# Attention with a gated token-mixing MLP on one core: rebuilding the prologue that leads to the first exponential

## The chip, the cores and the metric

The kernel runs on one core of one Trainium2 chip. The core has a matrix engine (TensorE, PE in the profile), a vector engine (VectorE, DVE), an activation engine (ScalarE, ACT), a general engine (GpSimd, POOL) and a queue engine that issues the transfers (SyncE, SP). The metric is the device time of one launch in microseconds; lower is better. Times given for the kernel are medians of several runs. The profile is one further execution.

## The reference

The input x has 2048 tokens of 640 features. It is normalized, goes through 32-head attention (20 features a head), and is multiplied by the SiLU of an MLP over the token axis, whose input is normalized once more:

```
xn  = layernorm(x)
qkv = xn @ wqkv                       # 32 heads, 20 features each
s   = softmax(q k^T / sqrt(20)) v @ wo
h   = layernorm(xn)                   # the second norm
u   = gelu(h^T @ w1 + b1)             # mixes tokens: 2048 -> 1536
y   = (u @ w2 + b2)^T                 # 1536 -> 2048
out = x + s * silu(y)
```

The scores are 32 x 2048 x 2048 numbers, and each needs an exponential. That is where the time of this kernel goes.

## The kernel before, in words

**Units.** The 32 heads go in eight groups G of four heads. In a group the queries go in four parts p of 512. One pass is one (G, p): 16 key blocks c of 128 keys times 4 heads g, 64 units. A unit is a score tile of 128 keys by 512 queries, so there are 2048 units. Four heads' scores can stand beside each other in TensorE, 32 rows each (L1024). A unit's exponential is taken either by ScalarE, two units at a time (L1051, 128 x 1024), or by VectorE as a chain of six instructions (L1091 to L1097, 128 x 512). The results are multiplied with the values (L1138) into one accumulator bank (bank 6), which a pass owns until its epilogue reads it (L1188). ScalarE's results stand in a ring of 24 tiles (`pt_sb`), VectorE's in one of 8.

**The prologue.** Before any score, x must be normalized. x is held in 16 blocks of 128 tokens, in four groups gb of four blocks. Per block there are two `bn_stats` (L545, L547) and one `bn_aggr` (L550) on VectorE; per group one addition of epsilon (L554) on VectorE, one power -0.5 on GpSimd over four columns (L557), and four normalizing instructions on VectorE (L560). Then TensorE transposes 20 tiles of 128 x 128 (L604) in three jobs of 2, 2 and 1 feature chunks; each job's bank is evicted to `xnT_sb` by VectorE (L949) or ScalarE (L948). With a group's transposed block the projections follow: keys of group G = 0 for 512 tokens (`k0_gb`, L622, evicted at L955 on ScalarE or L956 on VectorE), queries (`q0_0`, later `q0_1` to `q0_3`), and values in two jobs (`v0_...`, L674, evicted at L949). Scores of pass (0, 0) need `q0_0` and the key projection of their key block: each `k0_gb` opens 16 units, which are eight exponentials of ScalarE.

**The second norm.** Its row factor follows from the first one's statistics. Per group, GpSimd does five small instructions over four columns (L572 to L580, the fourth, L578, a power), and VectorE then writes the four blocks of h to `regC` (L583). All four groups do so after the last normalization (`xn_g3`). The MLP's first weights overwrite x in `regA`, so their load (`w1a`) waits for all of h.

**Constants.** VectorE fills the ones columns of the values and the gaps between them (L1213, L1215; `v_ones`), the store buffer `on_sb` (L1216) and a padded output weight (L1217), and writes the padding of the second query and key buffer (L1255), all in the prologue.

**What sets the order.** The instruction order of each engine is fixed when the program is built, by a planner in the same file. Work is given as jobs: a list of steps, the tags that must be done before (`requires`), and a priority (lower goes first). The planner keeps a model clock per engine with a cost for every step, always takes the engine whose next step can start first, and among steps ready then the one with the lowest priority number; evictions (`ev` steps) get 30 off theirs, scores have 0. An eviction may go to VectorE, or to ScalarE as well while the ramp lasts, that is until `v0_15` is done. VectorE's exponentials start only after that. Every engine runs its list strictly in order on the chip, so a step that is late there holds everything behind it.

A job that writes PSUM takes one of seven banks and holds it to its eviction. Once scores can start, banks 0 to 3 belong to ScalarE's exponentials, and three (4, 5, 7) are left to the prologue's jobs; at the end of the ramp 4 and 5 go to VectorE's exponentials. The jobs that want a bank stand in one queue, of which the planner looks at the first four. Later work (the other groups' key and query chunks, the MLP) is released by the number of the unit reached, not by time. Where TensorE would otherwise stand idle the planner puts in dummy multiplications (L1593, L1601).

**Loads.** All go through SP's queue in the order of the program, and rotate over eight lanes, each of which waits for its own transfer before. The first are x blocks 0, 1, 2-3, the first key and query columns, x blocks 4-7, the first value columns, x blocks 8-11 and 12-15 (`dma_x` L466, `dma_w` L471).

**The tail guard.** `DVE_TAIL_GUARD` keeps VectorE off the last units of a pass: it takes none of the last four. The same number sets how many units before the very end VectorE's banks are given up.

```
            if u < NU and u + len(dg) > pass_end[u] - self.DVE_TAIL_GUARD:
                u = pass_end[u]
```

## Time and profile before

| | us |
|---|---|
| median of 5 runs (873.74 to 875.24) | 874.17 |
| the profiled execution | 874.86 |
| its span | 872.7 |
| first exponential on ScalarE starts | 16.57 |
| first exponential step on VectorE starts (L1091) | 54.73 |
| ScalarE busy in the span | 842.5 |
| VectorE busy | 823.6 |
| TensorE busy (ends modelled, overlapping, dummies included) | 801.6 |

Busy time by stage, from the view that cuts the span into windows:

| window, us | TensorE | VectorE | ScalarE | GpSimd | GB/s |
|---|---|---|---|---|---|
| 0 to 5 | 2.83 | 3.81 | 1.28 | 0.74 | 154 |
| 5 to 10 | 3.13 | 3.98 | 0 | 1.02 | 304 |
| 10 to 15 | 4.26 | 4.90 | 2.29 | 0 | 366 |
| 15 to 20 | 4.97 | 3.65 | 3.69 | 1.01 | 197 |
| 20 to 30 | 8.55 | 8.62 | 9.06 | 1.44 | 95 |
| 30 to 40 | 8.57 | 8.20 | 7.34 | 2.70 | 7 |
| 40 to 50 | 8.06 | 8.70 | 7.41 | 6.48 | 2 |
| 50 to 60 | 9.74 | 6.13 | 8.78 | 0 | 197 |
| 60 to 80 | 18.81 | 19.83 | 20.00 | 0 | 29 |
| 800 to 850 | 44.14 | 47.84 | 49.83 | 0 | 26 |

How to read the profile: a group row gives line, engine, operation, output and input by name, shape, count, then busy time, mean nanoseconds of one, and the idle time of the engine just ahead of such instructions with what ended it. Records overlap, because an instruction's record begins before its predecessor's ends, so sums of records are somewhat longer than the engine's pace. In the timeline a row may merge several instructions; it gives start and duration, and in brackets the idle time before it. The chain of waits goes back from the last instruction to what released it each time.

### The profile page before, as it was taken

To read this page: it belongs to the slowest core of one execution; us is meant where nothing else is said; L and a number is where in the kernel's file an instruction comes from. 1 tells how busy PE (TensorE), PEld (TensorE's weight loads), DVE (VectorE), ACT (ScalarE), POOL (GpSimd) and SP (SyncE) were. 2 spreads that over 40 slices of the span, in tenths; PEclk is the share of its full clock that TensorE was granted. 3 is DMA by queue.
4 is the path that set the end of the run, shared out by engine and by line. 5 is a ranking of instruction groups with operands and counts; after the bars stand their busy time and mean duration, and the time that the engine had idled before them with its cause. 6 is when DMAs were issued, how large, how long until landed. Compare 5 with 4: busy or idle time off the path is not lost.

```text
span 872.7 us, 16547 instructions
## 1 busy us (share of the span) xinstructions
PE 801.6 (92%) x5814; PEld 260.0 (30%) x5908; DVE 823.6 (94%) x2048; ACT 842.5 (97%) x915; POOL 13.4 (2%) x31
## 2 busy tenths in 40 slices
PE   7889999999999999999999999999899999999897
PEld 4432222222332323232232223222222222222233
DVE  7979999999999999999999999999999999999997
ACT  4889999999999999999999999999999999999995
POOL 1310000000000000000000000000000000000000
PEclk9999999999999999999999999999999999999999
DMA  8140110010121213020013020222402210032111
GB/s 236 45 106 13 30 36 11 15 31 14 28 63 25 63 32 88 10 60 11 11 25 77 21 51 12 66 47 50 89 15 61 47 12 5 7 101 71 41 34 45
DMA packets 123286, 39.32 MB, mean 45 GB/s; under 512 B 84248, under 2 KB 122088, under 8 KB 123208
## 3 DMA queue, kind: packets, MB, share of 16 engines
q1 hardware_dynamic: 123208, 38.27, 19.2%
q8 instruction: 50, 0.82, 0.4%
q14 instruction: 28, 0.23, 0.1%
HBM read 25.88 MB, written 9.83 MB: 41 GB/s over the span
## 4 chain that ended last, share of the span: by engine, by line
ACT 84%; PE 8%; DVE 5%; POOL 1%; issue 1%; DMA 1%; SPq 0%; ACTq 0%; POOLq 0%; DVEq 0%
ACT pt_sb L1051 82%; PE ps_all L1024 3%; PE ps_all L1138 2%; PE ps_all L798 1%; ACT zt_sb L757 1%; ACT zt_sb L762 1%; POOL st_sb L578 1%; PE ps_all L1593 0%; PE ps_all L1601 0%; DMA regA<-in_A_x_dram 0%; PE ps_all L674 0%; PE ps_all L729 0%; DVE ew_sb L1091 0%; PE ps_all L622 0%; DVE dpt_sb L1097 0%
## 5 line engine op out<-in xcount | busy, mean ns | idle before, releaser
L1051 ACT ACTIVATE pt_sb<-ps_all 128x1024 bf16<-128x1024 f32 x889 | 821.4, 1124 | 7.6 <-PE ps_all L1024 6.8
L1024 PE MATMUL ps_all<-qk_sb 32*128 32x512 bf16 (+1 forms) x2112 | 368.9, 377 | 52.6 <-ACT pt_sb L1051 39.9
L1091 DVE TENSOR_SCALAR ew_sb<-ps_all 128x512 uint16<-128x512 uint16 x271 | 182.9, 684 | 23.8 <-PE ps_all L1024 22.8
L1024 PEld LDWEIGHTS ps_all<-qk_sb 32*128 32x128 bf16 x2112 | 97.7, 91 | 347.2 <-ACT pt_sb L1051 294.8
L1097 DVE SCALAR_TENSOR_TENSOR dpt_sb<-ps_all,el_sb 128x512 uint16<-128x512 f32 x271 | 180.5, 681 | 1.7
L1138 PE MATMUL ps_all<-pt_sb,v_sb 128*32 128x512 bf16 (+1 forms) x1834 | 163.9, 379 | 0.0
L1095 DVE TENSOR_TENSOR el_sb<-ev_sb,el_sb 128x512 bf16<-128x512 bf16 x271 | 109.3, 414 | 0.8
L1096 DVE TENSOR_TENSOR el_sb<-el_sb,ew_sb 128x512 bf16<-128x512 bf16 x271 | 108.8, 414 | 0.7
L1138 PE MATMUL ps_all<-dpt_sb,v_sb 128*32 128x512 bf16 (+1 forms) x278 | 85.4, 379 | 0.0
L729 PE MATMUL ps_all<-regB,regA 128*128 128x128 bf16 (+1 forms) x370 | 74.2, 299 | 2.6 <-issue 1.4
L1092 DVE TENSOR_SCALAR ev_sb<-ew_sb 128x512 bf16<-128x512 uint16 x271 | 74.2, 284 | 2.3
L729 PE MATMUL ps_all<-regC,regA 128*128 128x128 bf16 (+1 forms) x370 | 73.1, 299 | 1.4 <-issue 0.5
L1093 DVE TENSOR_SCALAR el_sb<-ew_sb 128x512 bf16<-128x512 uint16 x271 | 73.7, 282 | 0.0
L641 PE MATMUL ps_all<-xnT_sb,wqk_sb 128*112 128x512 bf16 x200 | 68.2, 405 | 1.0 <-DVE zt_sb L735 0.8
L1138 PEld LDWEIGHTS ps_all<-pt_sb,v_sb 128*32 128x32 bf16 x1834 | 36.6, 94 | 57.1 <-issue 50.0
L1593 PE MATMUL ps_all<-wrm_sb 128*128 128x512 bf16 (+1 forms) x139 | 41.1, 379 | 3.9 <-DVE ps_all L505 2.2
L729 PEld LDWEIGHTS ps_all<-regB,regA 128*128 128x128 bf16 x384 | 26.0, 97 | 38.3 <-issue 24.4
L729 PEld LDWEIGHTS ps_all<-regC,regA 128*128 128x128 bf16 x384 | 25.4, 97 | 38.1 <-issue 29.0
L674 PE MATMUL ps_all<-wv_sb,xnT_sb 128*128 128x160 bf16 (+1 forms) x160 | 34.0, 309 | 0.0
L798 PE MATMUL ps_all<-wo_sb,xnT_sb 128*128 128x128 bf16 (+2 forms) x152 | 30.8, 298 | 1.0 <-issue 0.9
L641 PEld LDWEIGHTS ps_all<-xnT_sb,wqk_sb 128*112 128x112 bf16 x200 | 21.7, 127 | 31.4 <-issue 13.2
L1601 PE MATMUL ps_all<-wrm_sb,v_sb 128*128 128x512 bf16 x76 | 27.2, 386 | 0.5 <-DVE rden_sb L1194 0.2
(79 smaller groups left out, 352.4 us busy)
## 6 DMA issues: line engine op xcount, KB each, us to landing
regA<-in_B_w_dram SPq DMA_DIRECT2D x6, 1024.0 KB
regA<-in_B_w_dram SPq DMA_DIRECT2D x8, 768.0 KB
regA<-in_A_x_dram SPq DMA_DIRECT2D x7, 640.0 KB
qkT_scratch_dram<-pk_sb SPq DMA_DIRECT2D x40, 112.0 KB
qk_sb<-qkT_scratch_dram SPq DMA_DIRECT2D x56, 80.0 KB
on_scratch_dram<-on_sb SPq DMA_DIRECT2D x124, 20.0 KB
out_dram<-regC SPq DMA_DIRECT2D x3, 640.0 KB
wqk_sb<-in_A_wqkv_dram SPq DMA_DIRECT2D x2, 680.0 KB
```

The lines of the kernel that those rows point to most:

```text
L641: steps.append(("pe", lambda e, dc=dc: e.matmul(ps_all[0:112, bk * 512:(bk + 1) * 512], wqk_sb[:, dc * 1280 + c0:dc * 1280 + c0 + 112], xn ...
L729: steps.append(("pe", lambda e, k=k: e.matmul(ps(bk, n), wap[:, k, col0:col0 + 128], rows[:, k, c0:c0 + n], start=(k == 0), stop=(k == nk ...
L1024: pr.pe(lambda e, outp=outp, lhsT=lhsT, rhs=rhs, g=g: e.matmul(outp, lhsT, rhs, start=True, stop=True, tile_position=(32 * g, 0)), reads=[ ...
L1051: tk = pr.act(lambda e: e.activation(outp, inp, AF.Exp, bias=-self.OFFS * math.log(2.0) / 128.0, scale=math.log(2.0) / 128.0), reads=[bank ...
L1091: (lambda e: e.tensor_scalar(w3, lo, 0x7FFF, None, ALU.bitwise_and), bs, [sw], dv(N)),
L1092: (lambda e: e.tensor_scalar(v_, w_, 1.0 / 256.0, -128.0, ALU.mult, ALU.add), [sw], [sv], dv(N, .26)),
L1093: (lambda e: e.tensor_scalar(l_, w_, a3 / 65536.0, (b3 - 64.0 * a3) / 256.0, ALU.mult, ALU.add), [sw], [sl_], dv(N, .26)),
L1095: (lambda e: e.tensor_tensor(l_, v_, l_, ALU.mult), [sv, sl_], [sl_], dv(N, .52)),
L1096: (lambda e: e.tensor_tensor(l_, l_, w_, ALU.mult), [sl_, sw], [sl_], dv(N, .52)),
L1097: (lambda e: e.scalar_tensor_tensor(o_, zr, -(self.OFFS - 16256.0), l_, ALU.add, ALU.add), bs + [sl_], [S_(f"dpt{s0 + i}") for i in range( ...
L1138: pr.pe(lambda e, outp=outp, lhsT=lhsT, rhs=rhs, k=k, g=g: e.matmul(outp, lhsT, rhs, start=(k == 0), stop=(k == NB - 1), tile_position=(0, ...
L1593: pe_full(lambda e: e.matmul(ps(wb, n), wrm_sb[:, 0:P], wrm_sb[:, P:P + n], start=True, stop=True), [S_("warm"), S_("warm1")], [bank_slot[ ...
```

## The change

- **Statistics.** Those of blocks 1 and 5 move to ScalarE (`act_stats`): an Identity with scale -1/640 whose accumulator gives the negative mean, a Square with that as bias whose accumulator gives the sum of squared deviations, and a one-column Copy that divides it by 640. Their element outputs go to `regC` as scrap. Since the mean is negative there, the two blocks' normalizations add it instead of subtracting. The rest of the statistics become jobs of their own (`stat0` to `stat3`), so that a group's statistics no longer wait for the normalization of the group before.
- **Loads.** x blocks 2 and 3 come by two transfers.
- **Group 0.** Its transposes are five jobs: for blocks 0 and 1 four chunks and one, for blocks 2 and 3 two, two and one. Queries 0 to 255 and keys 0 to 127 are projected after the first half, queries 256 to 511 and keys 128 to 511 after the second. The scores of key block 0 wait for all queries and the first key part only. The first value projections require that scores have begun (`STbegin0`).
- **Second norm.** One round of five GpSimd instructions over all 16 columns (`hstat`) instead of four rounds over four; the 16 VectorE writes of h have priority 88 (`H_PRIO`) instead of 32 to 35.
- **Constants.** The six fills go to GpSimd, ahead of all its powers. The padding of the second query and key buffer becomes a job of priority 60 after the last normalization.
- **Planner.** The model's cost of evicting a transposed block on VectorE is 0.55 ns an element instead of 1.04, and those of some small steps change; the tail guard is 3 instead of 4.

The diff, cut to its core:

```diff
     CHUNK_FROM = 44.0
+    ACT_STATS = (1, 5)
+    H_PRIO = 88.0
     DVE_EXP = True
-    DVE_TAIL_GUARD = 4
+    DVE_TAIL_GUARD = 3
     NTMP = 4
...
         dma_x(0, 1)
         dma_x(1, 1)
-        dma_x(2, 2)
+        dma_x(2, 1)
+        dma_x(3, 1)
...
+        def act_stats(b):
+
+            junk = regC[:, b, :]
+            nm, va = st_sb[:, 0, b:b + 1], st_sb[:, 1, b:b + 1]
+            return [("act", lambda e: e.activation(junk, regA[:, b, :], AF.Identity, scale=-1.0 / D, accum_out=nm),
+                     [S_(f"x{b}")], [S_(f"mv{b}"), S_(f"h{b}")], f"as0_{b}", ac(640)),
+                    ("act", lambda e: e.activation(junk, regA[:, b, :], AF.Square, bias=nm, accum_out=va),
+                     [S_(f"x{b}")], [S_(f"mv{b}"), S_(f"h{b}")], f"as1_{b}", ac(640) + 93.0),
+                    ("act", lambda e: e.activation(va, va, AF.Copy, scale=1.0 / D), [], [S_(f"mv{b}")], f"as2_{b}", 200.0)]
...
+        def stat_steps(gb):
+                if b in self.ACT_STATS:
+                    continue
...
+        def hstat_steps():
+
+            mvs = [S_(f"mv{b}") for b in range(NB)]
+            rs = [S_(f"rstd{gb}") for gb in range(4)]
+            sw, s3 = S_("lnw2"), S_("rr")
+            return [
+                ("pool", lambda e: e.tensor_tensor(st(5, 0, NB), st(2, 0, NB), st(2, 0, NB), ALU.mult), rs, [sw], "ha", 250.0),
+                ("pool", lambda e: e.tensor_tensor(st(5, 0, NB), st(5, 0, NB), st(1, 0, NB), ALU.mult), [sw] + mvs, [sw],
+                 "hb", 250.0),
+                ("pool", lambda e: e.tensor_scalar(st(5, 0, NB), st(5, 0, NB), self.EPS, None, ALU.add), [sw], [sw], "hc",
+                 300.0),
+                ("pool", lambda e: e.tensor_tensor(st(6, 0, NB), st(5, 0, NB), mhalf(NB), ALU.pow), [sw, S_("mhalf")],
+                 [S_("r2")], "hd", 1800.0),
+                ("pool", lambda e: e.tensor_tensor(st(3, 0, NB), st(2, 0, NB), st(6, 0, NB), ALU.mult), rs + [S_("r2")],
+                 [s3], "he", 250.0), ("tag", "hstat")]
...
+        def xT0_steps(half, dcs, nm):
+
+            def make(bk):
+                steps = []
+                pb = ps_all[:, bk * 512:(bk + 1) * 512].bitcast(bf)
+                for b in (2 * half, 2 * half + 1):
+                    for i, dc in enumerate(dcs):
+                        outp = pb[:, i * 256 + (b % 2) * 128:i * 256 + (b % 2 + 1) * 128]
+                        steps.append(("pe", lambda e, outp=outp, b=b, dc=dc: e.transpose(
+                            outp, xn_ap(b)[:, dc * 128:(dc + 1) * 128], idb_sb[:]),
+                            [S_(f"xn{b}"), S_("idb")], [bank_slot[bk]], "xT0", 128))
+                n = len(dcs)
+                dst = xnT_sb[:, dcs[0]:dcs[0] + n, half * 256:(half + 1) * 256]
+                src = pb[:, 0:n * 256].rearrange("p (c n) -> p c n", c=n)
+                steps.append(("ev", dst, src, "copy", None, [bank_slot[bk]], [S_(f"xT{dc}_0{half}") for dc in dcs],
+                              "xTe0", n * 256))
+                steps.append(("tag", f"xT0_{nm}"))
+                return steps
+            return make
...
+        def qk0_steps(w, c0, n, half, nm):
+
+            def make(bk):
+                steps = []
+                rd = [S_(f"wp{w}_0")] + [x for dc in range(5) for x in xsl(dc, 0, half)]
+                for dc in range(5):
+                    steps.append(("pe", lambda e, dc=dc: e.matmul(
+                        ps(bk, n), wqk0_sb[:, dc, w, :], xnT_sb[:, dc, c0:c0 + n], start=(dc == 0),
+                        stop=(dc == 4)), rd, [bank_slot[bk]], f"qk0_{w}_0{nm}", n))
+                steps.append(("ev", qk_sb[:, 0, w, c0:c0 + n], ps(bk, n), "k" if w else "q", None,
+                              [bank_slot[bk], S_("cq")], [S_(f"qkb0_{w}_0_{g}{nm}") for g in range(GH)], f"qke0_{w}_0{nm}", n))
+                steps.append(("tag", f"qk0_{w}_0{nm}"))
+                return steps
+            return make
...
+            if G == 0 and c == 0 and p == 0:
+                return "qk0_1_0a" in done and "qk0_0_0" in done
...
-        cs = []
         for h0, nh in ((0, 8), (8, 24)):
             onesap = bass.AP(v_sb, voff(h0), [[NB * VB, P], [VB, NB], [22, nh], [21, 2]])
-            cs.append(("dve", lambda e, ap=onesap: e.memset(ap, 1.0), [], [S_("v_ones")], "v_ones", 100.0 + NB * nh * 1.5))
+            pr.pool(lambda e, ap=onesap: e.memset(ap, 1.0), writes=[S_("v_ones")], name="v_ones", cost=100.0 + NB * nh * 1.7)
             gapap = bass.AP(v_sb, voff(h0 + nh - 1) + 22, [[NB * VB, P], [VB, NB], [1, 10]])
-            cs.append(("dve", lambda e, ap=gapap: e.memset(ap, 0.0), [], [S_("v_ones")], "v_gap", 150.0))
-        cs.append(("dve", lambda e: e.memset(on_sb[:], 0.0), [], [S_("on0"), S_("on1")], "on0", 290.0))
-        cs.append(("dve", lambda e: e.memset(wo7_sb[:], 0.0), [], [S_("wo7")], "wo70", 350.0))
-        cst2 = cs[2:]
-        add_job("consts", cs[:2] + [("tag", "c01")], ("ln_s0",), 20.8)
-        add_job("consts2", lambda bk: cst2 + [("tag", "consts")], ("xn_g1",), 24.5)
+            pr.pool(lambda e, ap=gapap: e.memset(ap, 0.0), writes=[S_("v_ones")], name="v_gap", cost=200.0)
+        pr.pool(lambda e: e.memset(on_sb[:], 0.0), writes=[S_("on0"), S_("on1")], name="on0", cost=900.0)
+        pr.pool(lambda e: e.memset(wo7_sb[:], 0.0), writes=[S_("wo7")], name="wo70", cost=600.0)
+        done.update(("consts", "c01"))
+        cst2 = []
+        XT0 = ("a", "b", "c", "d", "e")
+        add_job("consts2", lambda bk: cst2 + [("tag", "qpad")], ("xn_g3",), 60.0)
         for gb in range(4):
-            rq = () if gb == 0 else (f"xn_g{gb - 1}",)
-            if gb == 3:
-                rq = rq + tuple(f"xT0_{d}" for d in (0, 2, 4))
+            add_job(f"stat{gb}", stat_steps(gb), () if gb == 0 else (f"ln_s{gb - 1}",), 20.8 + gb)
+            rq = (f"ln_s{gb}",) + (() if gb < 3 else tuple(f"xT0_{d}" for d in XT0))
             add_job(f"ln{gb}", ln_steps(gb), rq, 20.0 + gb)
+        for b in self.ACT_STATS:
+            add_job(f"astat{b}", act_stats(b), (), 21.0 + b)
         add_job("wp0", [wp_step("dve", 1, 0, 250.0), wp_step("dve", 0, 0, 250.0), ("tag", "wpG0")], ("ln_s0",),
                 20.5)
-        add_job("h0", h_steps(0), ("xn_g0", "xn_g3"), 32.0)
-        add_job("h1", h_steps(1), ("h_g0",), 33.0)
-        add_job("h2", h_steps(2), ("h_g1",), 34.0)
-        add_job("h3", h_steps(3), ("h_g2",), 35.0)
+        add_job("hstat", hstat_steps(), ("xn_g3",), 40.0)
+        for gb in range(4):
+            add_job(f"h{gb}", h_steps(gb), ("hstat",), self.H_PRIO + gb / 10)
...
+        for nm, half, dcs in (("a", 0, (0, 1, 2, 3)), ("b", 0, (4,)), ("c", 1, (0, 1)), ("d", 1, (2, 3)), ("e", 1, (4,))):
+            add_bank_job(f"xT0_{nm}", xT0_steps(half, dcs, nm), (f"xn_b{2 * half + 1}",), 22.0)
+        h0_, h1_ = ("xT0_a", "xT0_b", "wpG0"), xts(0) + ("wpG0",)
+        add_bank_job("k0_0a", qk0_steps(1, 0, 128, 0, "a"), h0_, 22.1)
+        add_bank_job("q0_0a", qk0_steps(0, 0, 256, 0, "a"), h0_, 22.2)
+        add_bank_job("q0_0b", qk0_steps(0, 256, 256, 1, "b"), h1_, 22.3)
+        add_bank_job("k0_0b", qk0_steps(1, 128, 384, None, "b"), h1_, 22.4)
+        add_job("q0_0", [("tag", "qk0_0_0")], ("qk0_0_0a", "qk0_0_0b"))
+        add_job("k0_0", [("tag", "qk0_1_0")], ("qk0_1_0a", "qk0_1_0b"))
         for gb in range(4):
-            for dcs in ((0, 1), (2, 3), (4,)):
-                add_bank_job(f"xT{gb}_{dcs[0]}", xT_steps(gb, dcs), (f"xn_g{gb}",), 22.0 + gb)
-            add_bank_job(f"k0_{gb}", qk_steps(0, 1, gb), xts(4 * gb) + ("wpG0",), 22.5 + gb)
-            if gb == 0:
-                add_bank_job("q0_0", qk_steps(0, 0, 0), xts(0) + ("wpG0",), 22.6)
-            add_bank_job(f"v0_{4 * gb}", v_steps(4 * gb, 0), xts(4 * gb) + ("c01",), 23.0 + gb)
-            add_bank_job(f"v0_{4 * gb + 3}", v_steps(4 * gb + 3, 0), xts(4 * gb) + ("c01",), 23.0 + gb)
+            if gb:
+                for dcs in ((0, 1), (2, 3), (4,)):
+                    add_bank_job(f"xT{gb}_{dcs[0]}", xT_steps(gb, dcs), (f"xn_g{gb}",), 22.0 + gb)
+                add_bank_job(f"k0_{gb}", qk_steps(0, 1, gb), xts(4 * gb) + ("wpG0",), 22.5 + gb)
+            vq = xts(4 * gb) + ("STbegin0",)
+            add_bank_job(f"v0_{4 * gb}", v_steps(4 * gb, 0), vq, 23.0 + gb)
+            add_bank_job(f"v0_{4 * gb + 3}", v_steps(4 * gb + 3, 0), vq, 23.0 + gb)
...
-                rq = tuple(f"qkc{w}_{j}_{tb}" for j in range(c0 // 112, c1 // 112 + 1) for tb in range(NTB)) + ("consts",)
+                rq = tuple(f"qkc{w}_{j}_{tb}" for j in range(c0 // 112, c1 // 112 + 1) for tb in range(NTB)) + ("qpad",)
```

## The prediction

> **What bounds the kernel now.** I read the page first: what idle time the busiest engine has. Of the span, ScalarE's exponentials take most, and the last column of their row says how long ScalarE stood idle before one of them in the whole run.
>
> ```profile
> span 872.7 us, 16547 instructions
> ...
> L1051 ACT ACTIVATE pt_sb<-ps_all 128x1024 bf16<-128x1024 f32 x889 | 821.4, 1124 | 7.6 <-PE ps_all L1024 6.8
> ```
>
> So 889 exponentials wait 7.6 us in all. Their records overlap (mean 1124 ns); the chain's steps give the true pace, 50.67 us for 55, or 0.921 us each. Next, ScalarE's timeline over the first 60 us, to see where those 7.6 us lie (start, duration, group, then idle before it and its releaser).
>
> ```profile
> 11.34 1.51 ACT L948 ACTIVATE xnT_sb<-ps_all 128x1024 bf16<-128x1024 bf16 x2 [9.34 <-PE ps_all L604]
> ...
> 16.57 1.02 ACT L1051 ACTIVATE pt_sb<-ps_all 128x1024 bf16<-128x1024 f32 x1 [0.51 <-PE ps_all L1024]
> 18.11 3.00 ACT L1051 ACTIVATE pt_sb<-ps_all 128x1024 bf16<-128x1024 f32 x3 [0.52 <-PE ps_all L1024]
> ...
> 37.67 0.78 ACT L955 ACTIVATE qk_sb<-ps_all,cst_sb 128x512 bf16<-128x512 f32 x1 [2.04 <-PE ps_all L622]
> 38.93 4.80 ACT L1051 ACTIVATE pt_sb<-ps_all 128x1024 bf16<-128x1024 f32 x5 [0.49 <-PE ps_all L1024]
> ...
> 49.66 1.94 ACT L1051 ACTIVATE pt_sb<-ps_all 128x1024 bf16<-128x1024 f32 x2 [2.35 <-PE ps_all L1024]
> 52.68 7.75 ACT L1051 ACTIVATE pt_sb<-ps_all 128x1024 bf16<-128x1024 f32 x8 [1.08 <-PE ps_all L1024]
> ```
>
> The gaps after the first exponential (0.52, 0.44, 0.30, 2.04, 0.49, 0.23, 2.35, 1.08) sum to 7.45 us, all before 53 us; behind that ScalarE is never idle for more than tenths until 862.9. The time is an account of ScalarE: start 16.57, plus 889 x 0.921 = 818.8, idle 7.45, 14 tanh of 1.15 = 16.1, prologue evictions after the start some 3.2, makes 862.1 (the trace: 862.9), and a tail of 9.8 to 872.7. Nearly every microsecond of start or idle time that goes comes off the end. The large gaps sit where a new block of keys arrives (each 512-token projection opens 16 units, 8 exponentials); the chain, in order of time, says what those keys wait for.
>
> ```profile
> 1.65 3.89 DMA regA<-in_A_x_dram
> 5.56 0.49 DVE tr_sb L545
> ...
> 36.13 0.40 DVE tr_sb L547
> 37.05 1.01 POOL st_sb L557
> 39.06 1.09 POOL st_sb L578
> 41.36 1.20 POOL st_sb L578
> 43.65 1.17 POOL st_sb L578
> 46.19 1.08 POOL st_sb L578
> 47.58 0.80 DVE regC L583 x2
> 48.38 0.73 DVE qk_sb L956
> 49.16 0.75 PE ps_all L1024 x4
> ```
>
> VectorE's statistics lead to 36 us, then four rounds of GpSimd power operations for the second norm hold VectorE, in order, at L583; the key eviction L956 stands behind it and the exponential at 49.66 behind that. VectorE's own exponentials (271 units, about 2.98 us each between 54.7 and 861) begin only when the last value projection of the ramp is out:
>
> ```profile
> 53.06 0.89 DVE L949 CAST v_sb<-ps_all 128x480 bf16<-128x480 f32 x2 [3.25 <-PE ps_all L674]
> 54.73 0.69 DVE L1091 TENSOR_SCALAR ew_sb<-ps_all 128x512 uint16<-128x512 uint16 x1 [0.78 <-PE ps_all L1024]
> ```
>
> **The first exponential, part by part.** *Loads.* Blocks 2 and 3 come as two transfers, one issue more (0.4 us, as the 1.19 issue in the chain): all behind it on SP's queue is issued 0.4 us later. The bytes are the same. 154 GB/s over 0 to 5 us and 304 over 5 to 10 put blocks 4 to 7 at about 7.6 us, bandwidth-bound, so the issue costs nothing there; VectorE now reaches them about then, so up to 0.4 if that cover is gone. Block 2 lands earlier (about 4.7), block 3 at 5.6 to 6.0.
>
> *Statistics.* A block costs VectorE 1.05 us (starts 3.07 to 4.12, 5.56 to 6.61). Block 1 goes away: VectorE ends block 3 at about 6.9 instead of 7.7, so the power (1.02 on GpSimd) and the norm come 0.8 earlier. On ScalarE the block takes three dependent ACTIVATEs; evictions of 512 and 1024 columns took 0.60 and 1.02, so 640 is 0.71, with a bias pointer about 0.8, a 1-column one about 0.2: 1.7, up to 2.3 with the accumulator reads and waits that no row shows. ScalarE is idle to 11.34, and block 1 is there before 4.1, so it ends by 6.4, before VectorE's 6.9. Block 5 runs near 7.6 to 9.8 and can hold the first eviction by 0.5; taken below. [...] The row is one ACT_TABLE_LOAD of 1.28 us for Copy, Identity, Exp and Tanh. [...]
>
> *Memsets on GpSimd.* Six fills go ahead of the first power. GpSimd's 128x128 took 0.204 and 128x1 0.098: 0.83 ns an element. VectorE's rows have 2016 elements, since zeros went as uint32; [...] unpacked it is 3008. 2.3 or 3.1 us from 1.5: done by 4.6, before a power at 7. Cost 0; it would cost only from 5.5 us on. VectorE is rid of 2.0 us of fills.
>
> *Halves.* Before, the last norm ended at 10.79 and the first exponential came 5.8 us later: transposes to 11.64, evictions to 12.9, ten 512-column matmuls 2.32, two evictions of 0.78 in turn, scores. Now the norm ends at about 9.9, and behind it remain ten transposes already half done (0.5), the 512- and 256-column evictions on two engines (0.7), five 256-column matmuls (0.55 plus 0.3 of latency), a 256-column eviction (0.5), scores 0.4, hand-overs 0.2: 3.1 us. All 512 queries are still needed, so the last half counts. First exponential at 13.0, **3.6 earlier** (12.3 to 14.5). Four more evictions and ten more matmuls are 0.1 to 0.2 us each, in time where ScalarE was idle.
>
> **The gaps.** With the start at 13.0, gapless exponentials and about 1.3 us of evictions per block want keys 4-7 at 21.5, 8-11 at 30, 12-15 at 39. VectorE's work up to the last keys: 14 statistics 14.7, 16 norms of 0.36 = 5.8, weight copies 0.6, its share of transpose, key, query and value evictions 10 to 11: 32 from 3.07, with 2 to 4 of waits about 37 to 39. Gone are 2.1 of statistics, 2.0 of fills, and from ahead of the keys 1.4 of padding (L1255) and the second norm with its stalls (16 x 0.38 = 6.1). So keys come about when wanted: I take 2.5 us of gaps instead of 7.45, **-4.95** (0.8 to 6 left, as TensorE, busy 4.0 to 5.0 of each 5 us from 15 to 30, must also get denser). ScalarE takes perhaps 0.6 more of evictions, **+0.6** (0 to 2).
>
> *Second norm, late.* It is not free, its 6.1 us stay on VectorE, but they lie behind the evictions. One power of 16 columns replaces four of 4 (1.08 against 0.2 for a product): 1.1 if the cost is fixed, 3.7 if it goes by column; with four small ones 2.2 to 4.8 instead of 9.3. I take 3; what waits then is VectorE's exponentials and perhaps an eviction, up to 1.9. The MLP's first weights wait for the second norm, too (issued at 49.84); their first use is a hundred microseconds on. VectorE's exponentials start at about 47 (54.7 less 3.7 of work, less some 4 of its waits 3.25, 1.12, 0.85, 0.78), 7.7 earlier, and end some 7.9 earlier: the same 271 units, **0** (to 52: 1.7 units, 0.46 each, +0.8).
>
> *Tail guard 4 to 3.* VectorE may take a unit one place nearer a pass's end; 0, within 0.5 either way.
>
> Sum: -3.6 - 4.95 + 0.6 = -7.95 us. The profiled execution took 874.86 for a span of 872.7, the five timed runs 874.17 in the median. From the median: **866.2 us**; this case's own range is 863.5 to 869.
>
> **Rivals.** *Front only* (the gaps stay). Keys 12-15 come earlier only by the VectorE work removed, 3.7 us and a little, TensorE and the three free banks holding the rest: gain about 4, 870.2. For it speaks TensorE's load in that stretch; against, that the gaps at 37.67 and 49.66 hang on statistics and L583 by the chain. *All gaps go* and VectorE starts by 44: -3.6 - 6.9 - 0.5, 863.2; against it, the density of TensorE again. *Slower*: with guard 3 VectorE's last unit of a pass ends one place later, the accumulator is handed over late, the 24 score tiles fill and ScalarE stalls at each of 31 boundaries. From 0.25 us a boundary it eats the gain; at a full place (0.46) it gives 866.2 + 14.3 = 880.5. Against it: after 54 us ScalarE waited 0.9 us in all with guard 4, so the ring has room.
>
> **Numbers.** Main case 62 in 100, front only 20, all gaps 10, slower 5, and 3 where small losses cancel the gain. The range 862.4 to 871.0 leaves out the slow end, the cancelled case and the edges of two others. A measurement here tells 0.2% (1.7 us) from no change: faster 0.92, same 0.03, slower 0.05.
>
> **What would show it.** First exponential near 13.0; ScalarE's waits before exponentials 2 to 3 us; no ScalarE or VectorE group waiting for GpSimd's power more than 2 us; first L1091 successor near 47; still one table load; count near 889. Wrong if the key evictions still come near 38 and 49 us, or if ScalarE's idle time appears at pass ends.

## The result and the profile after

| | before | changed |
|---|---|---|
| median, us | 874.47 (75 runs, from 873.45) | 869.85 (40 runs, from 868.14) |
| ratio | | 0.9941 (0.9927 to 0.9955) |

The changed kernel is 4.6 us faster in the medians and 5.3 us faster in the best runs. The forecast was 866.2 us with a range of 862.4 to 871.0, so the time lies inside the range, 3.65 us above the forecast and outside the main case's own range (863.5 to 869): the width left for the other cases caught it, not the main case.

The execution that the profile of the changed kernel shows took 887.19 us and is not a typical one: TensorE ran at half its clock for 51 us in its middle, as shown below. Its first 60 us are undisturbed and are used here; the rest of the span is read from other profiles. The rows of the page that answer to those of before (the clock row has 40 slices of the span):

```profile
span 885.4 us, 16589 instructions
...
PEclk9999999999999999999999999999998559999999
...
L1129 ACT ACTIVATE pt_sb<-ps_all 128x1024 bf16<-128x1024 f32 x889 | 823.3, 1134 | 18.6 <-PE ps_all L1101 17.5
```

Still 889 exponentials on ScalarE and 271 chains on VectorE; the 18.6 us of waits are mostly the slow stretch. ScalarE's timeline of the prologue (start, duration, group, idle before it and its releaser):

```profile
9.40 0.74 ACT L549 ACTIVATE regC<-regA 128x640 bf16<-128x640 bf16 x1 [3.93 <-DMA regA<-in_A_x_dram]
10.05 0.19 ACT L549 ACTIVATION_READ_ACCUMULATOR regC<-regA 128x1 f32 x1
10.14 1.49 ACT L1023 ACTIVATE xnT_sb<-ps_all 128x1024 bf16<-128x1024 bf16 x2
...
14.19 0.67 ACT L1030 ACTIVATE qk_sb<-ps_all,cst_sb 128x384 bf16<-128x384 f32 x1 [0.80 <-PE ps_all L677]
14.76 7.71 ACT L1129 ACTIVATE pt_sb<-ps_all 128x1024 bf16<-128x1024 f32 x8
...
24.81 0.78 ACT L1030 ACTIVATE qk_sb<-ps_all,cst_sb 128x512 bf16<-128x512 f32 x1 [1.42 <-PE ps_all L697]
26.07 7.82 ACT L1129 ACTIVATE pt_sb<-ps_all 128x1024 bf16<-128x1024 f32 x8 [0.49 <-PE ps_all L1101]
34.17 0.78 ACT L1030 ACTIVATE qk_sb<-ps_all,cst_sb 128x512 bf16<-128x512 f32 x1 [0.28 <-PE ps_all L697]
35.44 1.94 ACT L1129 ACTIVATE pt_sb<-ps_all 128x1024 bf16<-128x1024 f32 x2 [0.48 <-PE ps_all L1101]
...
44.38 6.60 ACT L1129 ACTIVATE pt_sb<-ps_all 128x1024 bf16<-128x1024 f32 x7 [0.78 <-PE ps_all L1101]
```

The first exponential starts at 14.76 us (before 16.57). The gaps behind it are 1.42, 0.49, 0.28, 0.48, 0.16 and 0.78, in sum 3.61 us (before 7.45), and they end at 44.38 (before 52.68). Block 5's statistics wait for their transfer until 9.40, and the first eviction of transposed tiles, L1023, stands behind them in ScalarE's queue. TensorE's timeline of the same stretch:

```profile
8.95 1.52 PE L653 MATMUL ps_all<-idb_sb,regB 128*128 128x128 bf16 x20 [1.45 <-DVE regB L586]
11.29 2.86 PE L677 MATMUL ps_all<-xnT_sb,wqk_sb 128*128 128x128 bf16 x20 [0.81 <-ACT xnT_sb L1023]
```

The projections in halves run in one go of 20 matmuls, 2.86 us, behind the evictions of both halves; the two halves don't lie beside each other in time. VectorE and GpSimd at the end of the ramp:

```profile
30.65 1.51 DVE L586 TENSOR_SCALAR regB<-regA,st_sb 128x640 bf16<-128x640 bf16 x4
...
32.60 1.41 DVE L1344 TENSOR_SCALAR qk_sb<-wrm_sb,cst_sb 128x2048 bf16<-128x2048 bf16 x2
34.57 0.45 DVE L612 TENSOR_SCALAR regC<-regA,st_sb 128x640 bf16<-128x640 bf16 x1 [0.55 <-POOL st_sb L606]
...
40.97 1.86 DVE L612 TENSOR_SCALAR regC<-regA,st_sb 128x640 bf16<-128x640 bf16 x5
43.00 0.81 DVE L1031 TENSOR_SCALAR qk_sb<-ps_all,cst_sb 128x512 bf16<-128x512 f32 x1 [0.17 <-PE ps_all L697]
46.57 1.11 DVE L1024 CAST v_sb<-ps_all 128x480 bf16<-128x480 f32 x2 [2.75 <-PE ps_all L749]
48.14 1.32 DVE L1169 TENSOR_SCALAR ew_sb<-ps_all 128x512 uint16<-128x512 uint16 x2 [0.47 <-PE ps_all L1101]
```

```profile
2.63 2.23 POOL L1290 MEMSET v_sb<- 128x768 bf16 x1
...
7.32 1.10 POOL L583 TENSOR_TENSOR st_sb<-st_sb,cst_sb 128x4 f32<-128x4 f32 x1 [0.70 <-DVE st_sb L581]
...
31.23 3.00 POOL L604 TENSOR_TENSOR st_sb<-st_sb,cst_sb 128x16 f32<-128x16 f32 x1
```

The last normalization (L586) starts at 30.65, the last keys are evicted at 43.00 (L1031), and VectorE's exponentials start at 48.14 (before 54.73). VectorE waits 0.55 us for the second norm; the 16-column power takes 3.00 us. The same places in the profile of before, with two fills (L1213):

```profile
8.88 0.27 DVE L1213 MEMSET v_sb<- 128x256 bf16 x1 [0.47 <-issue]
...
21.30 0.70 DVE L1213 MEMSET v_sb<- 128x768 bf16 x1 [1.46 <-issue]
...
38.09 1.52 DVE L560 TENSOR_SCALAR regB<-regA,st_sb 128x640 bf16<-128x640 bf16 x4 [1.12 <-POOL st_sb L557]
...
47.58 0.80 DVE L583 TENSOR_SCALAR regC<-regA,st_sb 128x640 bf16<-128x640 bf16 x2 [0.85 <-POOL st_sb L580]
48.30 0.80 DVE L956 TENSOR_SCALAR qk_sb<-ps_all,cst_sb 128x512 bf16<-128x512 f32 x1
```

The last normalization comes 7.4 us earlier than before, the last keys 5.3 us earlier.

ScalarE's account, read from the timelines (the last column is a version from the experiments below, with two more edits):

| us | before | changed | changed, again | two edits more |
|---|---|---|---|---|
| span of the profiled execution | 872.7 | 885.4 | 872.7 | 865.5 |
| first exponential | 16.57 | 14.76 | 14.80 | 14.46 |
| gaps before 60 us | 7.45 | 3.61 | 3.62 | 3.61 |
| gaps after 60 us | 0.86 | 15.74 | 5.65 | 0.36 |
| last exponential's end to the end | 9.81 | 10.79 | 10.61 | 9.46 |

Start -1.8, gaps -3.8, tail +0.8 to +1.0: near -5, which is what the best runs differ by (868.14 to 873.45). The gaps after 60 us differ from execution to execution: nearly all of them in the two profiles of the changed kernel lie in stretches of half clock (681.7 to 732.9 us in the first, 820.8 to 834.5 in the second). Before has a short such stretch too, from 49.72 to 53.14 us, behind TensorE's wait of 1.89 us for the last keys: its last gap of the prologue, 1.08 at 52.68, lies in it.

### The profile page after: what moved, and what is told of

Same layout as the page of the kernel before. It is cut to its first block, busy times and chain, and to the rows that moved or that the text cites. A ratio compares the mean times of both kernels' runs of the same rounds, so it can differ in the third digit from the quotient of the medians.

```text
span 885.4 us, 16589 instructions
## 1 busy us (share of the span) xinstructions
PE 818.6 (92%) x5837; PEld 261.2 (29%) x5928; DVE 821.1 (93%) x2040; ACT 847.9 (96%) x925; POOL 13.9 (2%) x22
## 3 DMA queue, kind: packets, MB, share of 16 engines
q1 hardware_dynamic: 123224, 38.27, 18.6%
## 4 chain that ended last, share of the span: by engine, by line
ACT 81%; PE 14%; DVE 3%; DMA 1%; issue 1%; SPq 0%; DVEq 0%
ACT pt_sb L1129 79%; PE ps_all L1101 5%; PE ps_all L804 2%; PE ps_all L1216 2%; PE ps_all L1682 1%; PE ps_all L749 1%; ACT zt_sb L837 1%; PE ps_all L873 1%; DMA regA<-in_A_x_dram 1%; ACT zt_sb L832 1%; PE ps_all L697 1%; DVE ew_sb L1169 0%; PE ps_all L716 0%; DVE dpt_sb L1175 0%; PE ps_all L633 0%
## 5 line engine op out<-in xcount | busy, mean ns | idle before, releaser
L1129 ACT ACTIVATE pt_sb<-ps_all 128x1024 bf16<-128x1024 f32 x889 | 823.3, 1134 | 18.6 <-PE ps_all L1101 17.5
L1101 PE MATMUL ps_all<-qk_sb 32*128 32x512 bf16 (+1 forms) x2112 | 374.0, 386 | 50.8 <-ACT pt_sb L1129 40.7
L1216 PE MATMUL ps_all<-pt_sb,v_sb 128*32 128x512 bf16 (+1 forms) x1832 | 167.0, 387 | 0.3 <-DVE dpt_sb L1175 0.3
L804 PE MATMUL ps_all<-regB,regA 128*128 128x128 bf16 (+1 forms) x371 | 81.5, 319 | 1.6 <-issue 1.0
L716 PE MATMUL ps_all<-xnT_sb,wqk_sb 128*112 128x512 bf16 x200 | 66.4, 403 | 0.3 <-DVE el_sb L1174 0.2
L1682 PE MATMUL ps_all<-wrm_sb 128*128 128x512 bf16 (+1 forms) x145 | 46.7, 404 | 3.9 <-DVE ps_all L508 2.2
L873 PE MATMUL ps_all<-wo_sb,xnT_sb 128*128 128x128 bf16 (+2 forms) x154 | 30.9, 300 | 0.5 <-issue 0.3
```

What stands on the lines that cost most here:

```text
L716: steps.append(("pe", lambda e, dc=dc: e.matmul(ps_all[0:112, bk * 512:(bk + 1) * 512], wqk_sb[:, dc * 1280 + c0:dc * 1280 + c0 + 112], xn ...
L804: steps.append(("pe", lambda e, k=k: e.matmul(ps(bk, n), wap[:, k, col0:col0 + 128], rows[:, k, c0:c0 + n], start=(k == 0), stop=(k == nk ...
L1101: pr.pe(lambda e, outp=outp, lhsT=lhsT, rhs=rhs, g=g: e.matmul(outp, lhsT, rhs, start=True, stop=True, tile_position=(32 * g, 0)), reads=q ...
L1129: tk = pr.act(lambda e: e.activation(outp, inp, AF.Exp, bias=-self.OFFS * math.log(2.0) / 128.0, scale=math.log(2.0) / 128.0), reads=[bank ...
L1216: pr.pe(lambda e, outp=outp, lhsT=lhsT, rhs=rhs, k=k, g=g: e.matmul(outp, lhsT, rhs, start=(k == 0), stop=(k == NB - 1), tile_position=(0, ...
L1682: pe_full(lambda e: e.matmul(ps(wb, n), wrm_sb[:, 0:P], wrm_sb[:, P:P + n], start=True, stop=True), [S_("warm"), S_("warm1")], [bank_slot[ ...
```

## The experiments

My theory was the one of the prediction, in its account's terms: the start is worth what the first exponential moves, the gaps what the key evictions move, the second norm comes late for nothing. The rivals: that one part alone carries the gain, that the halves are the gain of the start, and that the missing 3.65 us are a new wait. The experiments were measured four at a time, beside runs of the kernel before: a median of 874.23 us for the first four, 875.3 for the second four and 875.21 for the last four. Line numbers in an experiment's lines are its own.

### The changed kernel once more

> The changed kernel itself, for a profile without the dip of the clock that the first one shows between 600 and 800 us. The account of ScalarE up to 53 us (start 14.76 instead of 16.57, idle 3.6 instead of 7.45, evictions 3.0 instead of 3.2) promises 5.8 us less than before. If nothing is lost later, the timed ratio gives 5.5 to 6 us and ScalarE's waits before its exponentials behind 54 us sum to under 1 us, as they did before. If part is given back later, the ratio stays near 0.994 (5 us) and these waits, or VectorE's count of units, show some 1 us.

Measured: 871.3 us median (868.48 to 887.88, 22 runs), ratio 0.9944 (0.9922 to 0.9966). The profiled execution, 874.54 us, has the same prologue (first exponential 14.80, gaps 3.62) and loses 5.3 us in one place, from 821 us on. TensorE's timeline there, and then the windows of one microsecond (busy time of TensorE, its weight loads, VectorE, ScalarE, GpSimd; then the granted clock, the share of the transfer engines, GB/s):

```profile
820.77 0.61 PE L873 MATMUL ps_all<-wo_sb,xnT_sb 128*128 128x512 bf16 x1 [1.72 <-DMA xnT_sb<-on_scratch_dram]
```

```profile
819.00:820.00 1.00, 0.05 (x2) 0.00 (x0) 1.00 (x4) 1.00 (x2) 0.00 (x0) 1.00 0.00 0
820.00:821.00 1.00, 0.23 (x1) 0.10 (x1) 0.06 (x1) 0.44 (x1) 0.00 (x0) 0.90 0.00 0
821.00:822.00 1.00, 1.00 (x4) 0.20 (x3) 0.58 (x1) 0.04 (x1) 0.00 (x0) 0.50 0.00 0
...
834.00:835.00 1.00, 0.98 (x4) 0.22 (x4) 0.29 (x1) 1.00 (x2) 0.00 (x0) 0.77 0.00 0
```

An output projection (L873) waits 1.72 us for the transposing reload of the attention output; then the clock is 0.50 from 820.8 to 834.5 and TensorE holds ScalarE: of the 5 us from 825 to 830 it is busy for 4.67, ScalarE for 3.54. The wait is not in the profile of before: its reload was issued at 819.51 and its first use came at 822.18, without a wait. So in this execution what lies above the best runs has its place at the end of the kernel.

### Blocks 4 to 7 in two transfers

```diff
-        dma_x(4, 4)
+        dma_x(4, 2, 655360)
+        dma_x(6, 2, 0)
```

(The third value is what the planner's model is told of the size, so that the order of the compute engines stays as it was.)

> x blocks 4 and 5 come by a transfer of their own ahead of 6 and 7; the order of instructions on all engines stays that of the changed kernel. Theory: the statistics of block 5 stand in ScalarE's queue ahead of the first eviction and wait for the four-block transfer until 9.40, which holds the projections to 11.3. Then block 5's Identity starts near 8.2, the first eviction near 9.6 (10.14), the first exponential at 14.0 to 14.3 (14.76), and the time is 0.4 to 0.7 us less than the changed kernel's. Rival: twenty short projections in a row and the evictions behind them set the start; then the first exponential stays at 14.6 to 14.8 and the time is the same.

Measured: 867.99 us (867.81 to 869.53, 6 runs), ratio 0.9915 (0.9882 to 0.9948). ScalarE's timeline:

```profile
8.36 0.74 ACT L549 ACTIVATE regC<-regA 128x640 bf16<-128x640 bf16 x1 [2.55 <-DMA regA<-in_A_x_dram]
...
9.72 1.51 ACT L1023 ACTIVATE xnT_sb<-ps_all 128x1024 bf16<-128x1024 bf16 x2 [0.54 <-PE ps_all L653]
...
14.38 7.71 ACT L1129 ACTIVATE pt_sb<-ps_all 128x1024 bf16<-128x1024 f32 x8
```

Block 5's statistics start 1.0 us earlier, the first eviction now waits for TensorE and not for a transfer, and the first exponential comes 0.4 us earlier. So block 5's statistics do hold the first eviction, and it costs 0.4 us. In this profile the reload's use at 818.69 found it there, with no wait. The median is 3.3 us below that of the unchanged kernel beside it, the best run 0.7; what the median holds beyond the 0.4 us is not shown, and the intervals of the two ratios overlap.

### One block's statistics on ScalarE

```diff
-    ACT_STATS = (1, 5)
+    ACT_STATS = (1,)
```

> Only block 1's statistics on ScalarE, block 5's back on VectorE (1.05 us more for it). Theory of the late block: ScalarE's queue has nothing to wait for, the first eviction starts near 9.4 and the first exponential at 13.2 to 13.8; the keys of group 1 come about 1 us later, so a gap there grows by up to 1 us; together 0 to 1 us less time than the changed kernel. Rival (VectorE's statistics are what counts): the second gap grows by more than the start gains, and the time is 0.5 to 1 us more.

Measured: 871.4 us (870.7 to 884.78, 22 runs), ratio 0.996 (0.9947 to 0.9973), beside 871.3 of the unchanged one. First exponential 14.00, gaps 4.49. Block 5's part of the change starts the exponentials 0.8 us later and takes 0.9 us of gaps away: an exchange, no gain that these runs can tell.

### The tail guard as it was

```diff
-    DVE_TAIL_GUARD = 3
+    DVE_TAIL_GUARD = 4
```

> The tail guard back at 4, all else as changed. The prediction gave this term 0, within 0.5 us either way; the prologue is the same to 60 us. The slower rival would have it that 3 costs at the ends of passes: then 4 is faster by 1 us or more, and the changed kernel shows ScalarE waits at the ends of passes that this one doesn't have.

Measured: 869.55 us (869.24 to 871.61, 11 runs), ratio 0.9939 (0.9918 to 0.996); 888 exponentials on ScalarE and 272 chains on VectorE. No difference that the medians or the intervals can tell; the best runs are 0.8 us apart, in favour of guard 3. ScalarE's gaps after 60 us are 1.35 us in all here, so with the guard at 4 or at 3 nothing collects at the ends of the passes, and the rival that ended slower is out. (In this profile TensorE had half its clock from 13.4 to 16.8 us and the first exponential came at 16.66; more on that below.)

### No statistics on ScalarE

```diff
-    ACT_STATS = (1, 5)
+    ACT_STATS = ()
```

> All 16 statistics on VectorE, the rest as changed. Prediction's view: VectorE has 2.1 us more ahead of the last keys, block 3's statistics end 0.8 later; the keys of 12 to 15 come 2 us later, ScalarE's gaps grow by about that; 1.5 to 2.5 us slower than the changed kernel. Rival: with block 5 gone from ScalarE's queue the first eviction no longer waits for the transfer that lands at 9.4, and the start (14.4 to 15.0) is as good as changed; moving statistics to ScalarE then brings under 1 us in all.

Measured: 878.71 us (872.99 to 1238.5, 22 runs), ratio 0.9998 (0.9966 to 1.003). The profile is that of the execution of 1238.5 us, in which TensorE's score multiplications took 520 ns in the mean over the whole span (386 in the changed kernel), so it says nothing of the prologue; the part is taken up again below.

### The fills back on VectorE

```diff
-            pr.pool(lambda e, ap=onesap: e.memset(ap, 1.0), writes=[S_("v_ones")], name="v_ones", cost=100.0 + NB * nh * 1.7)
+            cs.append(("dve", lambda e, ap=onesap: e.memset(ap, 1.0), [], [S_("v_ones")], "v_ones", 100.0 + NB * nh * 1.5))
...
+        add_job("consts", cs[:4] + [("tag", "c01")], ("ln_s0",), 20.8)
+        add_job("consts_b", lambda bk: cs2 + [("tag", "consts")], ("xn_g1",), 24.5)
```

(All six likewise; the four of the values go before the first norm, where two of them stood before the change, because the value projections now need all four.)

> The six fills back on VectorE (four behind the first group's statistics, two behind the second group's norm), 2.0 us of VectorE. If VectorE's work up to the keys sets the gaps, all 2.0 come back as later keys: 1 to 2 us slower than changed. Rival: the first four fall into VectorE's wait for the first power (0.85 us idle in the changed kernel at 7.6) and the others into waits for TensorE: under 0.7 us slower.

Measured: 873.55 us (872.11 to 877.89, 22 runs), ratio 0.9968 (0.9946 to 0.999). VectorE's timeline ahead of the first norm (L586):

```profile
7.21 0.15 DVE L581 TENSOR_SCALAR st_sb<-st_sb 128x4 f32<-128x4 f32 x1
...
8.10 0.27 DVE L1291 MEMSET v_sb<- 128x256 bf16 x1 [0.47 <-issue]
...
10.13 0.70 DVE L1291 MEMSET v_sb<- 128x768 bf16 x1 [1.55 <-issue]
10.59 1.45 DVE L586 TENSOR_SCALAR regB<-regA,st_sb 128x640 bf16<-128x640 bf16 x4
```

The norms start at 10.59 instead of 8.45, and TensorE's transposes at 11.04 instead of 8.95: 2.1 us. Only 1.1 us of it are the fills' records; 2.0 us are idle time just ahead of fills for which the profile shows no releaser (0.47 and 1.55), of which 0.85 replace a wait for the power that the changed kernel has there. The kernel before has the same idle time ahead of the same two fills (0.47 and 1.46). It grows with the fill, and with it the two cost 0.74 and 2.2 us here, about what they take on GpSimd (0.83 and 2.23); what it consists of isn't shown. The first exponential comes at 17.15, partly because TensorE's clock was 0.50 from 12.2 to 15.6 us in this profile; the gaps are 4.43. The result is worse than either expectation: by the ratios (0.9968 beside 0.9941, with intervals that overlap a little) about half of the change's gain hangs on this one part.

### Group 0 in one piece

```diff
-        for nm, half, dcs in (("a", 0, (0, 1, 2, 3)), ("b", 0, (4,)), ("c", 1, (0, 1)), ("d", 1, (2, 3)), ("e", 1, (4,))):
-            add_bank_job(f"xT0_{nm}", xT0_steps(half, dcs, nm), (f"xn_b{2 * half + 1}",), 22.0)
...
+        for nm, dcs in (("a", (0, 1)), ("b", (2, 3)), ("c", (4,))):
+            add_bank_job(f"xT0_{nm}", xT_steps(0, dcs, nm), ("xn_g0",), 22.0)
...
+        add_bank_job("k0_0", qk_steps(0, 1, 0), xts(0) + ("wpG0",), 22.5)
+        add_bank_job("q0_0", qk_steps(0, 0, 0), xts(0) + ("wpG0",), 22.6)
```

> Group 0 in whole again: three transpose jobs, one key and one query projection of 512. The prediction puts 2.8 of the 3.6 us of the start on the halves: the first exponential then comes near 16.5 to 17.5 instead of 14.8, and the time is 1.7 to 2.7 us longer. Rival: as all 512 queries are needed anyway the halves bring little: first exponential at 15 to 15.5, under 0.7 us longer.

Measured: 868.83 us (867.81 to 869.57, 6 runs), ratio 0.9895 (0.984 to 0.995), no slower than with halves. The first exponential comes at 16.45, though, 1.7 us later than in the changed kernel: here all of block 5's statistics stand ahead of ScalarE's first eviction, which starts at 11.68. The gaps are 4.73, those after 60 us 0.44. What is lost at the start is not seen in the time; a second pair of versions follows below.

### The second norm by groups

```diff
-        add_job("hstat", hstat_steps(), ("xn_g3",), 40.0)
-        for gb in range(4):
-            add_job(f"h{gb}", h_steps(gb), ("hstat",), self.H_PRIO + gb / 10)
+        add_job("h0", h_steps(0), ("xn_g0", "xn_g3"), 32.0)
+        add_job("h1", h_steps(1), ("h_g0",), 33.0)
+        add_job("h2", h_steps(2), ("h_g1",), 34.0)
+        add_job("h3", h_steps(3), ("h_g2",), 35.0)
```

(With `h_steps` as before the change: five GpSimd instructions over four columns for each group.)

> The second norm by groups again, right behind the last normalization, four rounds of five GpSimd instructions over four columns, priorities 32 to 35. By the chain before (L583 waiting for the power with the key eviction behind it) the last keys come 2 to 3 us later, with a gap near 46 us, and VectorE's exponentials start 2 us later: 1.5 to 3 us slower than changed. Rival: the planner fills the waits with other work and only the end of the ramp moves: under 1 us.

Measured: 876.51 us (872.11 to 879.99, 22 runs), ratio 0.9998 (0.9975 to 1.002). The gain is gone, but not where the expectation had put it. VectorE's timeline:

```profile
36.42 0.45 DVE L610 TENSOR_SCALAR regC<-regA,st_sb 128x640 bf16<-128x640 bf16 x1 [0.77 <-POOL st_sb L607]
...
38.89 1.51 DVE L610 TENSOR_SCALAR regC<-regA,st_sb 128x640 bf16<-128x640 bf16 x4 [0.35 <-POOL st_sb L607]
...
41.25 1.16 DVE L610 TENSOR_SCALAR regC<-regA,st_sb 128x640 bf16<-128x640 bf16 x3 [0.61 <-POOL st_sb L607]
...
45.40 0.81 DVE L1029 TENSOR_SCALAR qk_sb<-ps_all,cst_sb 128x512 bf16<-128x512 f32 x1
```

Three stalls of 1.73 us in sum take the place of one of 0.55, and the last keys come at 45.40 instead of 43.00. All 16 writes of h stand ahead of that eviction, as they do in the changed kernel too. The first exponential is 1.8 us later as well, so ScalarE's gaps in the prologue are 3.71 us, as in the changed kernel. What this execution loses is elsewhere: half clock in the prologue from 12.0 to 15.4 us (first exponential 16.54), and 6.3 us of gaps after 60 us, where the output projection waits 1.97 us for the reload and the clock is 0.50 from 824.4 to 831.2. Of its 22 runs, 18 took 875.55 us or more, with a mean clock over the span of 0.990 to 0.996; the four with a clock of 0.999 or 1.0 took 872.11 to 873.59, still above the changed kernel's 868.14 to 870.13 at such clocks. So the clock carries a part of the loss, but not all, and the rest has no place yet.

### The output projections later, and three combinations

```diff
-    OP_FROM = (1792.0, 1852.0, 1926.0)
+    OP_FROM = (1792.0, 1852.0, 1950.0)
```

> The changed kernel with the output projections of the third quarter of the tokens put 24 units later in the written order (OP_FROM 1926 to 1950); the prologue is untouched, only the order of the last 50 us differs, and one half exponential goes from ScalarE to VectorE. Theory 'late reload': the changed kernel's runs that lie 2 to 6 us above its best come from TensorE waiting 1 to 2 us at about 821 us for the transposing reload and then running at half clock; with the projections behind eight more P.V matmuls, that wait is 0 and no clock of 0.5 follows. Median 868.5 (868.0 to 869.2), hardly a run of 871 to 876; the ratio to before is 0.993. Rival 'it is something else': the same scatter, median 869.8, a third of the runs above 870.8, and a profile that can show half clock at 820 us without a wait before it.

Measured: 868.06 us (867.61 to 869.13, 6 runs), ratio 0.9914 (0.9887 to 0.9942). All six runs lie below 869.2, which of the unchanged kernel's 62 runs only 13 do; those were not made beside these, and the intervals of the ratios to before overlap. The reload's user still waits, 0.61 us in place of 1.72, and the clock stays whole behind it; ScalarE's gaps after 60 us are 0.36. The expectation of no wait at all was wrong, that of no slow clock held. The profiled execution took 869.0, a microsecond above the best, and shows where that went:

```profile
8.91 1.52 PE L653 MATMUL ps_all<-idb_sb,regB 128*128 128x128 bf16 x20 [1.81 <-DVE regB L586]
11.44 4.24 PE L677 MATMUL ps_all<-xnT_sb,wqk_sb 128*128 128x128 bf16 x20 [1.01 <-DVE tr_sb L566]
```

```profile
11.00:12.00 1.00, 0.56 (x5) 0.48 (x5) 0.44 (x2) 1.00 (x3) 0.00 (x0) 0.93 1.06 390
12.00:13.00 1.00, 1.00 (x7) 0.75 (x7) 0.76 (x3) 0.59 (x2) 0.00 (x0) 0.50 1.10 368
...
15.00:16.00 1.00, 1.00 (x6) 0.31 (x5) 0.96 (x5) 0.28 (x1) 0.00 (x0) 0.86 1.12 371
```

The same 20 projections as in the changed kernel take 4.24 us here instead of 2.86, at half the clock from 11.9 to 15.3 us, and the first exponential comes at 16.29. The written order up to there is the same in both.

**Both edits.** The two transfers and the later output projections together.

> Both single edits: x blocks 4, 5 and 6, 7 as two transfers, and the third quarter's output projections 24 units later. Theory: the start's gain of 0.4 us (first exponential at 14.4 instead of 14.8) and the missing reload wait add: median 868.0 (867.5 to 868.6), every undisturbed run below 869.6, ratio 0.992. Rival, that the small scatter of the split kernel was luck of six runs: median 869.5 and the scatter of the changed kernel.

Measured: 867.26 us (866.92 to 876.97, 14 runs, twelve of them between 866.92 and 867.39), ratio 0.9909 (0.9882 to 0.9937). First exponential 14.46, gaps 3.61 and 0.36, tail 9.46. This is the best version: its median is 2.6 us below that of the changed kernel, and twelve of its runs are below that kernel's best, 868.14. The two were not run side by side, and the intervals of their ratios to the kernel before overlap.

**Group 0 in one piece, with both edits.**

> Group 0 whole (three transposing jobs, one key and one query projection of 512 columns) with both single edits. Theory 'halves bring nothing to the end': first exponential about 16.0, gaps behind it 4.7 in place of 3.6, a shorter tail by about 1, together 868.3 (867.7 to 869.0), within 0.6 us of the version with halves. Rival 'halves are worth what the first exponential shows': 1.6 us slower than the version with halves, 869.6 or more.

Measured: 869.17 us (868.06 to 872.16, 7 runs), ratio 0.9926 (0.99 to 0.9952). Beside the version with halves it is slower by 0.5 us in the profiled executions (866.0 to 865.5). The accounts say how that is made up: start 15.33 against 14.46, gaps 4.73 against 3.61, one exponential fewer on ScalarE (-0.9), and less eviction work and pace behind it. TensorE's and ScalarE's rows:

```profile
11.71 2.32 PE L697 MATMUL ps_all<-xnT_sb,wqk_sb 128*128 128x512 bf16 x10 [0.72 <-ACT xnT_sb L1023]
```

```profile
14.07 0.78 ACT L1030 ACTIVATE qk_sb<-ps_all,cst_sb 128x512 bf16<-128x512 f32 x1 [0.30 <-PE ps_all L697]
15.33 1.94 ACT L1129 ACTIVATE pt_sb<-ps_all 128x1024 bf16<-128x1024 f32 x2 [0.48 <-PE ps_all L1101]
```

So the halves bring the start forward by 0.9 us in this pair and by 1.7 in the one above, not by the 2.7 that the prediction made of them. Here they are worth 0.5 us by the profiles, 1.1 by the best runs (868.06 to 866.92) and 1.9 by the medians; without the two edits the version in one piece was no slower, though it was not measured beside the changed kernel. What they are worth to the end is therefore not settled.

**No statistics on ScalarE, with the later output projections.**

> All sixteen blocks' statistics on VectorE, all else as changed, with the later output projections. Theory: ScalarE's statistics are worth the 1.0 us by which VectorE's norms would end later, and the second norm is late anyway: first exponential at 15.5 to 16.0, gaps 3.6 to 4.5, time 869.7 (868.8 to 870.6), 1 us above the changed kernel with the same late edit. Rival 'the statistics carry the gain': 872 to 874, the time of before. Second rival, since one block's statistics alone began the exponentials sooner than two: equal to the changed kernel, 868.5.

Measured: 873.33 us (872.57 to 875.98, 22 runs), ratio 0.9974 (0.9959 to 0.9989), 5.3 us above the same kernel with the statistics. The theory was wrong and the rival was right in its number: with the runs of one block above, most of the gain hangs on one block or none on ScalarE, and nothing that shows on one or two. VectorE's timeline shows the start of it:

```profile
9.98 0.49 DVE L564 BATCH_NORM_STATS2 tr_sb<-regA 128x6 f32<-128x320 bf16 x1 [1.47 <-DMA regA<-in_A_x_dram]
10.39 1.50 DVE L586 TENSOR_SCALAR regB<-regA,st_sb 128x640 bf16<-128x640 bf16 x4
```

Group 0's four statistics are done at 7.25, hardly later than in the changed kernel (6.94). But in the new written order block 4's first statistic (L564) stands ahead of group 0's norm (L586), and it waits until 9.98 for its transfer; the norm follows at 10.39 instead of 8.45. The planner believes that transfer to be there earlier than it is. The loss at the start (0.7 us at the first exponential) is therefore not the work of a block's statistics, some 1.05 us, but a place in a queue. The profiled executions differ by 5.0 us: 0.7 at the first exponential (both at half clock there), 2.6 in gaps after 60 us, 0.8 in the tail, 1.8 in ScalarE's eviction work and pace, less 0.9 for an exponential fewer. Why the gaps after 60 us (seven of 0.2 to 0.6 us between 80 and 781) and the slower pace come with it isn't shown: the planner writes the whole order anew. So the run shows that the edit costs 5.3 us, and explains 0.7 of them.

## Why the prediction was right, and where it was off

- **Direction and range: right, with some luck.** The account of ScalarE was the right instrument: start, gaps and tail add up to what the best runs differ by. The forecast of -7.95 us was 3 us too good, and both large terms of it came out smaller, the second of them by another mechanism than the one given.
- **First exponential at 13.0: wrong, 14.76.** Of 3.6 us came 1.8. The norms end at 9.96, as predicted (9.9). The step that failed is "behind it remain ... 3.1 us"; it measured 4.80. Transposes 0.51 (predicted 0.5); then to the start of the projections at 11.29 0.82 (evictions, predicted 0.7); then to the eviction of the last queries at 13.36 2.07 (predicted 0.85, one half's matmuls: 0.55, and 0.3 of latency, an estimate; before, the first projection's eviction came 1.28 after the first of its five 512-column matmuls, which at their pace of 0.216 leaves 0.20); that eviction, scores and hand-overs to 14.47 1.11 (predicted 1.1); and 0.29 more because the eviction of the other keys, L1030 at 14.19, stands ahead of the exponential on ScalarE. What I missed is that the first half's 1024 columns are out only at about 11.1, when VectorE's share of the second half is out as well and ScalarE's follows within 0.6 us, so that all 20 projections come in one piece, longer than before (2.86 to 2.32). The versions in one piece show the same from the other side: the halves move the start by 0.9 us, or by 1.7 where block 5's statistics come first.
- **Transfers at about 7.6: wrong.** Block 5's landed by 9.40, and by 9.1 to 10.1 in the other profiles where blocks 4 to 7 come by one transfer (8.4 where by two). I had named what this does, "can hold the first eviction by 0.5; taken below", and then didn't put it into the sum. Two transfers took 0.4 of it back.
- **Gaps 7.45 to 2.5: 3.61, near in size, but not by the mechanism given.** The term was 3.84 instead of 4.95. The step that failed is "gone ... from ahead of the keys 1.4 of padding (L1255) and the second norm with its stalls". They are not gone from there: the padding (32.60) and all 16 writes of h (34.57 to 42.83) still stand ahead of the last keys' eviction at 43.00. They only no longer hold it: it waits 0.17 us for TensorE, while before, the keys were projected by 46.8 and their eviction stood behind h until 48.30. Nor were the stalls large: of the four powers in the chain VectorE waited for one, 0.85 us.
- **What did move the gaps, as far as the records show it.** VectorE comes to its last normalization 7.4 us earlier. What was taken off ahead of it adds up to about that: 2.1 us of statistics, 1.4 of padding, 2.0 of fills, and 1.9 of idle time ahead of two fills, which the prediction didn't count. This is a sum, not an experiment. Moved back one at a time, one block's statistics brought back 0.9 us of gaps, the fills 0.8, the whole group 0 1.1, the norm by groups 0.1, and all the statistics, with the later output projections, 0.05: none brings back the 3.84. The padding, the statistics as jobs of their own and the planner's new costs were not tried alone, and 1.08 of the 7.45 lay in a stretch of half clock. Of the 3.61 left, 1.91 stand at keys 4 to 7, whose blocks are normalized no earlier than before (from 17.79, before 17.55).
- **Second norm late, 0: right in the prologue, not shown beyond it.** The power took 3.00 us (I took 3), VectorE waited 0.55 (up to 1.9), its exponentials start at 48.14 (about 47). Moving it back cost the whole gain in the median, in part by way of TensorE's clock.
- **Evictions +0.6: too much.** Between the accounts 0.0 is left over for the changed kernel's second profile and -0.4 for the version with two more edits.
- **Fills on GpSimd, 0: right, with the duration wrong.** I had put them at 2.3 to 3.1 us, done by 4.6; they end at 6.6. The 128x768 one took 2.23 us, 2.9 ns an element, where the 128x128 row had given 0.83; the contiguous 128x1024 took 0.95 us. The cost would begin where the first power stands, and that waited for VectorE to 7.32: 0.7 us of cover are left. What the fills free on VectorE was put too low, at 2.0 us: with the idle time ahead of two of them it is 3.95.
- **Statistics on ScalarE: right.** ScalarE's rows of the changed kernel show one ACT_TABLE_LOAD, 1.28 us at 0.72, and those of before the same: Square did not bring another. Block 1 took 0.74 + 0.19 + 0.83 + 0.19 + 0.20, 2.0 us from 3.45 to 5.47, between my 1.7 and 2.3; the accumulator reads are instructions of their own.
- **Tail guard, 0 within 0.5: right,** as far as the runs can tell.
- **What the sum left out.** The tail behind the last exponential grew by 0.8 to 1.0 us in the two profiles of the changed kernel, and runs with a lower mean clock took longer: 868.14 to 870.13 us at a clock of 0.998 or more, 874.28 to 874.82 at 0.992 to 0.994. I had neither in the prediction. The rival *front only* is nearest in time (870.2 to 869.85), and its mechanism is refuted: the gaps shrank by 3.84 us, and the front fell short.

## What to carry to other kernels

Splitting a job in two halves gains only what the second half no longer waits for: check at each engine in between (here one eviction of 1024 columns) that the first half is really through before the second arrives. In an order written out by hand, an instruction that waits for a transfer holds everything behind it, so put work on late blocks behind the work that is ready, whatever the model of the transfer says; here such a place moved the first normalization from 8.45 to 10.39 us. Count the idle time ahead of an instruction with its cost: two fills that took 1.0 us by their records took 2.9 of the queue. And when the bound engine lives from another engine being dense, a wait on that other engine can cost several times its length (1.72 us of TensorE's brought 5.3 us of ScalarE's gaps).
